# Attention and two dense layers on one core: another way to turn the first two score blocks of the last six jobs

## The chip, the cores and the metric

One core of one Trainium2 chip runs the kernel. The metric is the device time of one execution in microseconds (us), lower being better; the kernel before has a median of 1113.16 us.

## What is computed

```python
def _attn_ref(q, k, v, tau):                  # q, k, v: 4 x 8 x 576 x 64, fp32
    scores = (1.0 / np.sqrt(64)) * np.matmul(q, k.transpose(0, 1, 3, 2))
    thresh = np.max(scores, axis=-1, keepdims=True) - tau
    scores = np.where(scores >= thresh, scores, -1000000000.0)
    scores = scores - np.max(scores, axis=-1, keepdims=True)
    attn = np.exp(scores)
    attn = attn / (np.sum(attn, axis=-1, keepdims=True) + 1e-09)
    return np.matmul(attn, v)
# x = heads joined, 2304 x 512;  then twice  x = g(x @ w_in) @ w_out,  d_ff = 2048
# first g: 0 below -1, (h+1)^2/4 between, h above 1;  second g: h * clip(h + 3, 0, 6) / 6
```

## The kernel before

**Jobs and blocks.** Attention runs in 16 jobs, each a pair of heads of one batch row. The code counts them from 0, so jobs eleven to sixteen are `j` = 10 to 15; this text uses the code's numbers. A job has five blocks of queries: four of 128 per head, and a last one with the 64 remaining queries of both heads. From the moment the first batch row is ready, the matmuls of the first dense layer (`em_h`, line 742, and `em_part`, line 804) are interleaved with the attention steps, so TensorE has two kinds of work in its queue.

**One step of a block.** `em_scores` (line 352) makes the scores on TensorE in two pairs of PSUM banks. VectorE takes them out (line 391): it multiplies by a negative scalar, clips, and gives the row minimum `nm` of the negated scores. `em_exp` (line 398) makes `e = exp(nm - p)` on ScalarE for each head, and then the threshold `th = nm + tau` (line 407) on VectorE. `em_mask` (line 409) compares `p` with `th`, multiplies by `e` and sums, on VectorE (line 413). The masked block must then be turned, keys onto partitions, before the product with v (`pv_chunk`, lines 483 to 502).

**From job 10 on** (`JR = JD = 10`) two things differ. First, the queries and keys come in by strips, are transposed by VectorE in 32 x 32 pieces into a tile `raw` (line 300), split by ScalarE into a rounded part (`qt`, `kt`, line 301) and by GpSimd into the rest (`ql`, `kl`, line 302); scores are the sum of three products. The scale 1/8 is put on with the scalar `taus[:, 3:4]` at line 392. Second, blocks 0 and 1 of a job are turned by `place` (line 426): VectorE transposes 32 x 32 pieces of the block into `pb`, with a strided order of input and output (line 433), and four DMAs per head move the pieces to the tile `Gf` (line 438), 16 DMAs per job. Blocks 2 to 4 are turned by TensorE and copied by ScalarE. `chunk` (line 440) picks the 128 keys of one chunk out of `Gf`; the matmul at line 496 multiplies them with the matching rows of `vn`.

**Buffers.** The tag `w_raw` has three buffers (`RAW = 3`). They hold raw weights, the tiles `raw` and the tiles `kl`. The tag `w_more` has two, for `ql`. `pb` takes the tag `w_c`, two buffers, which the weight preparation also uses. `kt` and `qt` have two buffers each.

**Order.** All DMAs but a few at the start are sent by the queue of SyncE (SP), in order. The plan in `attention` (lines 575 to 690) asks for the queries of job j+1 at block 3 of job j (`unit_q`), for its keys at block 4 (`unit_k`), and for the loads of the next ones behind them. The order within an engine's queue is then fixed by the framework's scheduler when the program is built, from priorities and a timeline that it estimates; in the trace work often runs earlier than the plan names it.

Of the kernel before, what the change touches and what calls it, by code (L numbers as in the profile page):

```python
# [8 lines left out]
F32 = mybir.dt.float32  # L9
# [9 lines left out]
def kernel(  # L19
# [234 lines left out]
    def load_k(j):  # L254
        if j >= NJ:
            return
        b, hp = jobs[j]
        for h in HEADS:
            src = k[b, 2 * hp + h]
            if j >= JT:  # L260
                strips(kn, 2, src, h)
                strips(kn, 0, src[MAIN:SEQ, :], h)
                continue
            nc.sync.dma_start(out=kn[:, 0:4, h * D:(h + 1) * D], in_=rows(src, b))
        if j < JT:
            for r in range(2):
                nc.sync.dma_start(out=kn[r * TAIL:(r + 1) * TAIL, 4, :].rearrange("p (h d) -> p h d", h=2),
                                  in_=both(k, j))
# [24 lines left out]

    def spare(name, tag):
        pool, n = (ap, MORE) if tag == "w_more" else (stage, RAW)
        return pool.tile([128, 1024], F32 if name == "raw" else F32R, tag=tag, name=name, bufs=n)[:, 0:SEQ + TAIL]

    def split_t(nat, hi, name, raw):
        lo = spare(name, "w_more" if name == "ql" else "w_raw")
        V.transpose(out=raw, in_=nat.rearrange("p c n -> p (c n)"))  # L300
        S.activation(out=hi, in_=raw, func=ACTF.Copy)
        G.tensor_tensor(out=lo, in0=raw, in1=f32(hi), op=ALU.subtract)
        return lo
# [3 lines left out]
    def unit_q(j):  # L307
        if j >= NJ or j in qt:
            return
        qt[j] = ap.tile([128, SEQ + TAIL], F32R if j >= JR else F32, tag="qt", name="qt", bufs=2)  # L310
        if j >= JR:
            raws[j] = spare("raw", "w_raw")
            ql[j] = split_t(qn, qt[j], "ql", raws[j])
            load_q(j + 1)
            return
        if j >= JT:
            V.transpose(out=qt[j][:, 0:SEQ], in_=qn.rearrange("p c n -> p (c n)")[:, 0:SEQ])
            if j == JR - 1:
                G.memset(qn[0:64, 4, 64:128], 0.0)
                G.memset(qn[64:128, 4, 0:64], 0.0)  # L320
            load_q(j + 1)
            G.tensor_scalar(out=qt[j][:, 0:SEQ], in0=qt[j][:, 0:SEQ], scalar1=taus[:, 1:2], scalar2=None, op0=ALU.mult)
            return
        tm = unit_bank().rearrange("p e n -> p (e n)")
        for c in range(5):
            turn(tm[:, c * 128:(c + 1) * 128], qn[:, c, :], c == 0)
        load_q(j + 1)
        reads(S.activation(out=qt[j][:, 0:SEQ], in_=tm[:, 0:SEQ], func=ACTF.Copy, scale=taus[:, 1:2]))

    def unit_k(j):  # L330

        if j >= NJ or j in kt:
            return
        kt[j] = ap.tile([128, SEQ + TAIL], F32R if j >= JR else F32, tag="kt", name="kt", bufs=2)
        if j >= JR:
            kl[j] = split_t(kn, kt[j], "kl", raws.pop(j))
            load_k(j + 1)
            return
        if j >= JT:
            V.transpose(out=kt[j], in_=kn.rearrange("p c n -> p (c n)"))  # L340
            load_k(j + 1)
            return
        tm = unit_bank().rearrange("p e n -> p (e n)")
        for i, c in enumerate((4, 0, 1, 2, 3, 4)):
            turn(tm[:, i * 128:(i + 1) * 128], kn[:, c, :], i == 0)
        load_k(j + 1)
        reads(S.activation(out=kt[j], in_=tm[:, 128 - TAIL:128 + MAIN + TAIL], func=ACTF.Copy))
# [4 lines left out]
    def em_scores(j, i):  # L352
# [36 lines left out]
            zt[j] = ap.tile([128, 9], F32, tag="z", name="z", bufs=2)  # L389
        for x, s in enumerate(ss):  # L390
            reads(V.tensor_scalar(out=p[:, x], in0=s[:, :, 0:HS],  # L391
                                           scalar1=taus[:, 3:4] if j >= JR else -1.0, scalar2=3e38,
                                           op0=ALU.mult, op1=ALU.min, accum_out=nm[:, x:x + 1]), len(ss) - 1 - x)
        blk[j, i] = (p, nm, th, [])

# [2 lines left out]
    def em_exp(j, i, x):  # L398
        p, nm, th, es = blk[j, i]
        n = 1 if i == NBLK - 1 else 2  # L400
        if x >= n:
            return
        e = ap.tile([128, 2, HS], F32, tag="e", name="e", bufs=3)
        pins["S"] = S.activation(out=e, in_=p[:, x], func=ACTF.Exp, bias=nm[:, x:x + 1], scale=-1.0)  # L404
        es.append(e)
        if x == n - 1:
            V.tensor_scalar(out=th[:, 0:n], in0=nm[:, 0:n], scalar1=taus[:, 0:1], scalar2=None, op0=ALU.add)

    def em_mask(j, i):
# [16 lines left out]
    def place(j, i):  # L426

        p = p_t[j, i]
        f = turned(j, "a")[0].rearrange("p h c n -> p h (c n)")
        for h in HEADS:  # L430
            p0 = h * (SEQ + TAIL)
            y = stage.tile([128, MAIN], F32, tag="w_c", name="pb", bufs=2)
            V.transpose(out=y.rearrange("p (g c k) -> p g c k", g=4, c=4),  # L433
                        in_=p[:, p0:p0 + MAIN].rearrange("p (c k g) -> p g c k", c=4, g=4))
            for a in range(4):
                c = (4 * i + a) * 128
                E = nc.sync
                E.dma_start(out=f[:, h, c:c + 128], in_=y[32 * a:32 * a + 32, :].rearrange("k (g x) -> k g x", g=4))  # L438

    def chunk(f, j, g, h, c):  # L440
        if j >= JD and g == "a":
            return f[:, h].rearrange("p c n -> p (c n)").rearrange("p (s c n) -> p c s n", c=4, n=32)[:, c]
        return f[:, h, c]

    def rotate():
        mode["r"] = 1 - mode.get("r", 0)
# [36 lines left out]
    def pv_chunk():  # L483

        j, g, c = pvq.pop(0)
        n, d0 = GROUPS[g]
        f, t = gt[g, j]
        if c == 0:
            if j not in xu:
                here.pop(j - XLIVE, None)  # L490
                xu[j] = here[j] = mt.tile([128, SEQ], F32, tag="xu", name="xu", bufs=XLIVE)
            o_t[j, g] = rotate() if mode["mlp"] else bank("Q1")
        o = o_t[j, g][:, 0:n]
        for h in (1, 0):
            with tc.high_priority(offset=0 if h else 900):
                mm = T.matmul(o[h * D:(h + 1) * D], vn[j % 2][:, c, h, :], chunk(f, j, g, h, c) if c < 4 else t,  # L496
                              start=(c == 0), stop=(c == 4), skip_group_check=True)
            after(mm, pe_pins[-1] if h else prev)
            prev = mm
        if c == 4:  # L500
            del gt[g, j], o_t[j, g]
            S.activation(out=xu[j][:, d0:d0 + n], in_=o, func=ACTF.Copy)
# [459 lines left out]
    V.tensor_scalar(out=taus[:, 3:4], in0=taus[:, 2:3], scalar1=0.0, scalar2=3e38, op0=ALU.is_lt, op1=ALU.mult)  # L962
    V.tensor_scalar(out=taus[:, 1:2], in0=taus[:, 2:3], scalar1=0.0, scalar2=0.125, op0=ALU.is_ge, op1=ALU.mult)
    V.tensor_tensor(out=taus[:, 0:1], in0=taus[:, 2:3], in1=taus[:, 3:4], op=ALU.max)
    V.tensor_scalar(out=taus[:, 3:4], in0=taus[:, 1:2], scalar1=-1.0, scalar2=None, op0=ALU.mult)
    warm = [None]

    def warm_up(n):
# [150 lines left out]
```

## Time and profile before

| | us |
|---|---|
| median of three runs | 1113.16 (1112.78 to 1113.59) |
| profiled execution, whole time | 1114.19 |
| its span, first to last instruction | 1112.4 |
| TensorE busy | 1072.6 (96%) |
| VectorE busy | 613.9 (55%) |
| ScalarE busy | 608.4 (55%) |
| GpSimd busy | 453.1 (41%) |

PE is TensorE's matmuls and PEld its weight loads, DVE is VectorE, ACT ScalarE, POOL GpSimd, SPq the queue from which SyncE sends DMAs. The shares are averages over unlike stages: attention with the first dense layer runs to about 445 us, and what comes after it is dense layers alone. The stage of the change is that of jobs 10 to 15, from about 270 to 445 us. An idle time of an engine is put down to the instruction that released it last.

### The profile page before, as it was taken

What the parts mean: (1) busy time and instruction counts of PE and PEld (TensorE: products, weight loads), DVE (VectorE), ACT (ScalarE), POOL (GpSimd) and SP (SyncE); (2) the same over time, 40 slices, a digit from 0 to 9 for tenths busy, and PEclk for the clock granted to TensorE, in tenths of its full rate; (3) what the DMA queues carried; (4) which work ended last, traced back from release to release, by engine and by line L of the source; (5) the groups of instructions that cost most, each with busy time, mean ns of one, the idle gap of its engine ahead of it and who ended that gap; (6) DMA issues with size and microseconds to landing.
All of it is one profiled execution on the core that took longest, in us unless ns stands there. A gap on an engine that the chain in (4) does not pass through costs nothing.

```text
span 1112.4 us, 17797 instructions
## 1 busy us (share of the span) xinstructions
PE 1072.6 (96%) x6466; PEld 880.1 (79%) x6466; DVE 613.9 (55%) x1229; ACT 608.4 (55%) x1203; POOL 453.1 (41%) x390
## 2 busy tenths in 40 slices
PE   7988889999999999999999999999999999999998
PEld 5555567778877788988899888888888888898886
DVE  5889988975889986454437765557411111211111
ACT  5777886876655666565557766645422232333222
POOL 0233767732332312374627566667522222222221
PEclk9999899999999999999999999999999999999999
DMA  6445545332444343143223445533010110010001
GB/s 170 119 96 108 126 115 138 69 86 72 101 98 101 85 106 83 39 121 116 78 76 95 150 147 155 150 120 96 24 38 1 34 39 1 10 39 10 10 1 38
DMA packets 154440, 90.57 MB, mean 81 GB/s; under 512 B 101360, under 2 KB 137456, under 8 KB 154352
## 3 DMA queue, kind: packets, MB, share of 16 engines
q1 hardware_dynamic: 153008, 89.14, 29.8%
q8 instruction: 51, 0.84, 0.3%
q10 hardware_dynamic: 1344, 0.30, 0.1%
q14 instruction: 37, 0.30, 0.1%
HBM read 65.73 MB, written 17.37 MB: 75 GB/s over the span
## 4 chain that ended last, share of the span: by engine, by line
PE 80%; DVE 10%; ACT 3%; issue 2%; SPq 2%; DMA 2%; POOL 1%; DVEq 0%; POOLq 0%; ACTq 0%
PE Q L742 33%; PE P L784 28%; PE Q L804 6%; PE Q L496 5%; PE P L376 4%; DVE p L391 3%; PE Q L290 3%; DVE p L413 3%; DMA Gf<-pb 1%; SPq L438 1%; DVE pb L433 1%; ACT e L404 1%; DVE xl L723 1%; SPq L229 1%; DVE w_c L137 0%
## 5 line engine op out<-in xcount | busy, mean ns | idle before, releaser
L760 POOL TENSOR_TENSOR gl<-r,gh 128x512 fp32r<-128x512 f32 (+1 forms) x190 | 206.6, 1087 | 461.1 <-ACT gh L759 446.4
L742 PE MATMUL Q<-xh,wih 128*128 128x512 f32 (+1 forms) x760 | 260.1, 343 | 1.2 <-DVE r L753 1.1
L742 PE MATMUL Q<-xl,wih 128*128 128x512 f32 (+1 forms) x760 | 256.9, 338 | 0.0
L742 PE MATMUL Q<-xh,wil 128*128 128x512 f32 (+1 forms) x760 | 256.6, 338 | 0.0
L756 DVE SCALAR_TENSOR_TENSOR r<-r,Q 128x512 f32<-128x512 f32 (+1 forms) x80 | 50.7, 633 | 249.4 <-ACT r L755 249.3
L759 ACT ACTIVATE gh<-r 128x512 fp32r<-128x512 f32 (+1 forms) x190 | 99.9, 526 | 138.5 <-PE P L784 53.2
L742 PEld LDWEIGHTS Q<-xh,wih 128*128 128x128 f32 x760 | 144.2, 190 | 22.9 <-issue 2.8
L742 PEld LDWEIGHTS Q<-xl,wih 128*128 128x128 f32 x760 | 144.2, 190 | 15.7
L742 PEld LDWEIGHTS Q<-xh,wil 128*128 128x128 f32 x760 | 144.0, 189 | 15.4
L404 ACT ACTIVATE e<-p,nm 128x576 f32<-128x576 f32 x144 | 109.6, 775 | 49.8 <-DVE p L391 49.3
L413 DVE SCALAR_TENSOR_TENSOR p<-p,th,e 128x576 f32<-128x576 f32 x144 | 125.9, 895 | 14.3 <-ACT e L404 8.3
L755 ACT ACTIVATE r<-Q,three 128x512 f32<-128x512 f32 (+1 forms) x80 | 51.4, 643 | 143.8 <-PE Q L742 140.7
L753 DVE SCALAR_TENSOR_TENSOR r<-r,Q 128x256 f32<-128x256 f32 (+1 forms) x110 | 54.7, 497 | 114.0 <-ACT r L752 112.7
L784 PE MATMUL P<-woh,gh 128*128 128x512 f32 x288 | 111.9, 390 | 0.6 <-DVE ob L842 0.6
L784 PE MATMUL P<-wol,gh 128*128 128x512 f32 x288 | 112.3, 390 | 0.0
L784 PE MATMUL P<-woh,gl 128*128 128x512 f32 x288 | 111.0, 390 | 0.0
L139 POOL TENSOR_TENSOR w_c<-w_c,w_raw 128x512 int32<-128x512 int32 x64 | 89.2, 1394 | 38.1 <-DVE w_c L137 21.7
L290 PE MATMUL Q<-ident,p 128*128 128x128 f32 x560 | 91.8, 282 | 11.6 <-ACT Gf L460 7.0
L376 PE MATMUL P<-kt,qt 64*128 64x288 f32 (+2 forms) x508 | 84.7, 420 | 16.5 <-DVE p L391 14.5
L290 PEld LDWEIGHTS Q<-ident,p 128*128 128x128 f32 x560 | 63.2, 141 | 40.6 <-ACT Gf L460 13.1
L751 ACT ACTIVATE r<-Q,half 128x256 f32<-128x256 f32 (+1 forms) x110 | 58.7, 535 | 41.5 <-PE Q L742 32.7
L804 PE MATMUL Q<-gh,woh 128*128 128x256 f32 x240 | 75.1, 313 | 1.4 <-DVE ob L817 1.4
(107 smaller groups left out, 1978.5 us busy)
## 6 DMA issues: line engine op xcount, KB each, us to landing
w_raw<-in_moe_w_in_dram SPq DMA_DIRECT2D x32, 512.0 KB
w_raw<-in_moe_w_out_dram SPq DMA_DIRECT2D x32, 512.0 KB
Gf<-pb SPq DMA_DIRECT2D x96, 64.0 KB
vn<-in_v_dram SPq DMA_DIRECT2D x32, 128.0 KB
x2p<-ob SPq DMA_DIRECT2D x16, 256.0 KB
x2d<-ob SPq DMA_DIRECT2D x16, 256.0 KB
xst<-x2d SPq DMA_DIRECT2D x16, 256.0 KB
out_dram<-ob SPq DMA_DIRECT2D x16, 256.0 KB
```

Source lines behind the costliest of these rows:

```text
L139: x = G.tensor_tensor(out=c.bitcast(I32), in0=c.bitcast(I32), in1=r, op=ALU.add)
L290: x = T.transpose(out, in_, ident)
L376: mm = T.matmul(o, a[j][r, cs], w[j][r, k0:k0 + HS], start=(n == 0), stop=(n == len(terms) - 1), skip_group_check=True)
L404: pins["S"] = S.activation(out=e, in_=p[:, x], func=ACTF.Exp, bias=nm[:, x:x + 1], scale=-1.0)
L413: pins["M"] = V.scalar_tensor_tensor(out=p[:, x], in0=p[:, x], scalar=th[:, x:x + 1], in1=e, op0=ALU.is_le, op1=ALU.mult, accum_out=zt[j][ ...
L496: mm = T.matmul(o[h * D:(h + 1) * D], vn[j % 2][:, c, h, :], chunk(f, j, g, h, c) if c < 4 else t, start=(c == 0), stop=(c == 4), skip_gro ...
L742: mm = T.matmul(h, l[:, kk * 128:(kk + 1) * 128], r, start=(x == 0), stop=(x == 3 * KD - 1))
L751: S.activation(out=r, in_=h, func=ACTF.Relu, scale=0.5, bias=half)
L759: x = S.activation(out=gh, in_=r, func=ACTF.Copy)
L760: y = G.tensor_tensor(out=gl, in0=r, in1=f32(gh), op=ALU.subtract)
L784: T.matmul(a, l, r, start=(first and x == 0), stop=(last and x == 2))
L804: mm = T.matmul(o, l, r, start=(f == fs[0] and x == 0 and i == 0), stop=(f == fs[-1] and x == 2 and i == 1), skip_group_check=True)
```

## The change

It has four parts, all for jobs 10 to 15.

1. `place` transposes the block without strides. The pieces therefore hold other keys: chunk c of the first group (blocks 0 and 1) now has the keys in another order, and needs rows of v in that order. A second copy of v, `vps`, is loaded for it, by two DMAs per job, into the upper half (columns 512 to 1023) of the job's `raw` tile; the load stands in `unit_k`, behind the load of the next keys.
2. The first of the four `pb` tiles of a job lies in the lower half of the same `raw` tile, and no longer in a `w_c` buffer. The `raw` tile is thereby held until the product with v has read `vps`, where it was free before once `kl` was made.
3. ScalarE multiplies the raw queries by 1/8 in place, before the split; line 391 multiplies by the constant -1.0 in place of the per-partition scalar, and the instruction that made that scalar goes.
4. The threshold `th` is made by ScalarE (`Identity` with a bias), behind the two exponentials, in place of VectorE.

```diff
-        return pool.tile([128, 1024], F32 if name == "raw" else F32R, ...)[:, 0:SEQ + TAIL]
+        return pool.tile([128, 1024], F32, tag=tag, name=name, bufs=n)
-    def split_t(nat, hi, name, raw):
-        lo = spare(name, "w_more" if name == "ql" else "w_raw")
+    vps = {}
+    def split_t(j, nat, hi, name, whole):
+        t = spare(name, "w_more" if name == "ql" else "w_raw")
+        lo = t[:, 0:SEQ + TAIL].bitcast(F32R)
+        raw = whole[:, 0:SEQ + TAIL]
         V.transpose(out=raw, in_=nat.rearrange("p c n -> p (c n)"))
+        if name == "ql":
+            S.activation(out=raw, in_=raw, func=ACTF.Copy, scale=taus[:, 1:2])
         S.activation(out=hi, in_=raw, func=ACTF.Copy)
         G.tensor_tensor(out=lo, in0=raw, in1=f32(hi), op=ALU.subtract)
...
-            kl[j] = split_t(kn, kt[j], "kl", raws.pop(j))
+            kl[j] = split_t(j, kn, kt[j], "kl", raws[j])
             load_k(j + 1)
+            b, hp = jobs[j]
+            vps[j] = raws[j][:, MAIN:2 * MAIN].rearrange("p (h c d) -> p h c d", h=2, c=4)
+            for h in HEADS:
+                nc.sync.dma_start(out=vps[j][:, h], in_=v[b, 2 * hp + h][0:MAIN, :].rearrange("(a c k) d -> k a c d", a=4, c=4))
...
-                                           scalar1=taus[:, 3:4] if j >= JR else -1.0, scalar2=3e38,
+                                           scalar1=-1.0, scalar2=3e38,
...
-        if x == n - 1:
+        if x == n - 1 and j >= JD:
+            S.activation(out=th[:, 0:n], in_=nm[:, 0:n], func=ACTF.Identity, bias=taus[:, 0:1])
+        elif x == n - 1:
             V.tensor_scalar(out=th[:, 0:n], in0=nm[:, 0:n], scalar1=taus[:, 0:1], scalar2=None, op0=ALU.add)
...
-            y = stage.tile([128, MAIN], F32, tag="w_c", name="pb", bufs=2)
-            V.transpose(out=y.rearrange("p (g c k) -> p g c k", g=4, c=4),
-                        in_=p[:, p0:p0 + MAIN].rearrange("p (c k g) -> p g c k", c=4, g=4))
+            if i or h:
+                y = stage.tile([128, MAIN], F32, tag="w_c", name="pb", bufs=2)
+            else:
+                y = raws[j][:, 0:MAIN]
+            V.transpose(out=y, in_=p[:, p0:p0 + MAIN])
...
+    def chunk(j, g, h, c):
+        f, t = gt[g, j]
+        if c == 4:
+            return vn[j % 2][:, c, h, :], t
         if j >= JD and g == "a":
-            return f[:, h].rearrange(...)[:, c]
-        return f[:, h, c]
+            return (vps[j][:, h, c, :],
+                    f[:, h].rearrange("p c n -> p (c n)").rearrange("p (s c n) -> p c s n", c=4, n=32)[:, c])
+        return vn[j % 2][:, c, h, :], f[:, h, c]
...
-    V.tensor_scalar(out=taus[:, 3:4], in0=taus[:, 1:2], scalar1=-1.0, scalar2=None, op0=ALU.mult)
```

## Rows read from the trace of the kernel before

**Rows 1.** Busy time by stretch: length; PE, PEld, DVE, ACT, POOL; clock; DMA share, GB/s.

```profile
303.00:330.00 27.00, 24.66 (x201) 20.80 (x201) 23.42 (x56) 15.87 (x36) 7.17 (x6) 0.94 0.43 98
275.00:411.00 136.00, 126.92 (x1062) 106.97 (x1060) 120.72 (x278) 86.24 (x192) 38.60 (x33) 0.99 0.43 97
411.00:445.00 34.00, 32.62 (x274) 28.22 (x272) 23.40 (x56) 23.15 (x54) 6.22 (x8) 1.00 0.33 88
445.00:1000.00 555.00, 555.00 (x2829) 474.14 (x2826) 229.60 (x316) 266.98 (x477) 254.76 (x205) 1.00 0.24 77
```

**Rows 2.** Waits of TensorE and VectorE, 270 to 445 us: total, times, longest.

```profile
PE P L376 <- DVE p L391: 5.0, 4, 2.3
PE Q L496 <- DMA Gf<-pb: 2.4, 3, 1.0
PE Q L290 <- DVE p L413: 1.0, 2, 0.8
DVE pb L433 <- DMA Gf<-pb: 6.7, 4, 2.1
DVE p L413 <- ACT e L404: 3.9, 7, 1.0
```

**Rows 3.** Timeline of job 11, VectorE and TensorE: start, length, what, idle before.

```profile
317.10 1.08 DVE L433 STREAM_TRANSPOSE pb<-p 128x512 f32<-128x512 f32 x1 [2.15 <-DMA Gf<-pb]
318.93 0.40 PE L376 MATMUL P<-kt,qt 64*128 64x288 f32 x2 [2.34 <-DVE p L391]
```

**Rows 4.** VectorE's groups by shape: busy, mean ns, idle before; 270 to 445 us.

```profile
L391 DVE TENSOR_SCALAR_CACHE_REDUCE p<-P,taus 128x576 f32<-128x576 f32 x54 | 42.1, 808 | 6.0 <-PE Q L290 3.5 <-PE P L376 2.4
L433 DVE STREAM_TRANSPOSE pb<-p 128x512 f32<-128x512 f32 x24 | 26.2, 1111 | 6.7 <-DMA Gf<-pb 6.7
L407 DVE TENSOR_SCALAR th<-nm,taus 128x2 f32<-128x2 f32 x24 | 6.2, 259 | 0.5
L300 DVE STREAM_TRANSPOSE raw<-kn 128x640 f32<-128x640 f32 x5 | 4.2, 839 | 0.9 <-DMA kn<-in_k_dram 0.7 <-issue 0.2
L407 DVE TENSOR_SCALAR th<-nm,taus 128x1 f32<-128x1 f32 x6 | 1.3, 209 | 0.0
```

**Rows 5.** The same groups over the whole run, jobs 0 to 9 among them.

```profile
L391 DVE TENSOR_SCALAR_CACHE_REDUCE p<-P 128x576 f32<-128x576 f32 x90 | 65.2, 751 | 18.9 <-PE Q L290 11.2 <-PE P L376 6.7
L317 DVE STREAM_TRANSPOSE qt<-qn 128x576 f32<-128x576 f32 x6 | 4.6, 772 | 1.1 <-DMA qn<-in_q_dram 1.1
```

**Rows 6.** ScalarE's groups, 270 to 445 us, and its one table load.

```profile
L404 ACT ACTIVATE e<-p,nm 128x576 f32<-128x576 f32 x54 | 41.3, 774 | 22.2 <-DVE p L391 22.1
L474 ACT ACTIVATE Gt<-Q 128x128 f32<-128x128 f32 x26 | 6.9, 267 | 0.9 <-PE Q L290 0.9
L301 ACT ACTIVATE qt<-raw 128x640 fp32r<-128x640 f32 x4 | 2.9, 725 | 0.0
L961 ACT ACT_TABLE_LOAD x1 | 1.3, 1283 | 3.4 <-issue 3.4
```

**Rows 7.** SP's queue: one line's loads, two stretches of job 11, its waits there.

```profile
L277 SPq DMA_DIRECT2D vn<-in_v_dram x14: 372/537/583, 226.6 to 407.2; - x14
...
312.81 5.12 SPq L438 DMA_DIRECT2D Gf<-pb  x8
...
318.67 5.11 SPq L438 DMA_DIRECT2D Gf<-pb  x8
...
SPq L438 <- DVE p L413: 0.6, 1, 0.6
...
SPq L818 <- DVE pb L433: 0.2, 1, 0.2
```

**Rows 8.** Timeline at the change from job 10 to job 11: GpSimd, then TensorE.

```profile
271.46 1.55 POOL L302 TENSOR_TENSOR kl<-raw,kt 128x640 fp32r<-128x640 f32 x1 [1.53 <-ACT kt L301]
295.00 0.30 PE L376 MATMUL P<-kt,ql 128*128 128x288 f32 x1
299.27 0.40 PE L376 MATMUL P<-kt,qt 64*128 64x288 f32 x2
```

More of the change, by code (lines that the diff above doesn't have):

```diff
@@ L295, in spare @@
         pool, n = (ap, MORE) if tag == "w_more" else (stage, RAW)
-        return pool.tile([128, 1024], F32 if name == "raw" else F32R, tag=tag, name=name, bufs=n)[:, 0:SEQ + TAIL]
-    def split_t(nat, hi, name, raw):
-        lo = spare(name, "w_more" if name == "ql" else "w_raw")
+        return pool.tile([128, 1024], F32, tag=tag, name=name, bufs=n)
[4 more added lines that the diff above has]
+        raw = whole[:, 0:SEQ + TAIL]
         V.transpose(out=raw, in_=nat.rearrange("p c n -> p (c n)"))
+        if name == "ql":
+            S.activation(out=raw, in_=raw, func=ACTF.Copy, scale=taus[:, 1:2])
         S.activation(out=hi, in_=raw, func=ACTF.Copy)
@@ L312, in unit_q @@
             raws[j] = spare("raw", "w_raw")
-            ql[j] = split_t(qn, qt[j], "ql", raws[j])
+            ql[j] = split_t(j, qn, qt[j], "ql", raws[j])
             load_q(j + 1)
@@ L431, in place @@
             p0 = h * (SEQ + TAIL)
-            y = stage.tile([128, MAIN], F32, tag="w_c", name="pb", bufs=2)
-            V.transpose(out=y.rearrange("p (g c k) -> p g c k", g=4, c=4),
-                        in_=p[:, p0:p0 + MAIN].rearrange("p (c k g) -> p g c k", c=4, g=4))
+            if i or h:
[3 more added lines that the diff above has]
+            V.transpose(out=y, in_=p[:, p0:p0 + MAIN])
             for a in range(4):
                 c = (4 * i + a) * 128
-                E = nc.sync
-                E.dma_start(out=f[:, h, c:c + 128], in_=y[32 * a:32 * a + 32, :].rearrange("k (g x) -> k g x", g=4))
-    def chunk(f, j, g, h, c):
+                nc.sync.dma_start(out=f[:, h, c:c + 128], in_=y[32 * a:32 * a + 32, :].rearrange("k (g x) -> k g x", g=4))
+    def chunk(j, g, h, c):
+        f, t = gt[g, j]
+        if c == 4:
+            return vn[j % 2][:, c, h, :], t
         if j >= JD and g == "a":
-            return f[:, h].rearrange("p c n -> p (c n)").rearrange("p (s c n) -> p c s n", c=4, n=32)[:, c]
-        return f[:, h, c]
+            return (vps[j][:, h, c, :],
+                    f[:, h].rearrange("p c n -> p (c n)").rearrange("p (s c n) -> p c s n", c=4, n=32)[:, c])
+        return vn[j % 2][:, c, h, :], f[:, h, c]
     def rotate():
@@ L495, in pv_chunk @@
             with tc.high_priority(offset=0 if h else 900):
-                mm = T.matmul(o[h * D:(h + 1) * D], vn[j % 2][:, c, h, :], chunk(f, j, g, h, c) if c < 4 else t,
+                mm = T.matmul(o[h * D:(h + 1) * D], *chunk(j, g, h, c),
                               start=(c == 0), stop=(c == 4), skip_group_check=True)
```

## The prediction

> **What bounds the kernel now.** I read the busy times by stretch first [rows 1]. From 445 to 1000 us TensorE is busy for the whole 555.00 us: nothing that the change does to other engines can show there. In the stretch of the change it isn't: 126.92 of 136.00 us (275 to 411) and 32.62 of 34.00 (411 to 445), so 9.1 + 1.4 = 10.5 us are idle. That is the most that better feeding can give back, and it is small. One thing comes on top: from 303 to 330 the mean granted clock is 0.94 of the upper level (2.4 GHz), against 1.00 in the last two stretches; 6% of 27 us is 1.6 us, which lie in the busy time.
>
> Next the waits [rows 2]: who caused those 10.5 us. 5.0 us are scores that wait for VectorE to empty their PSUM banks (line 391), 1.0 us turns that wait for masks (line 413), and 2.4 us products with v that wait for the last DMA of `place`. The rest (2.1 us) is not touched here. VectorE in its turn stands still for 6.7 us, four times, before the transpose of line 433, because a `pb` buffer is not free until its DMAs have landed. Job 11 shows the chain [rows 3]: the third transpose waits 2.15 us for the first one's buffer, and the scores behind it wait 2.34 us.
>
> So in this stage three queues run close to each other: TensorE busy 93%, VectorE 120.72 of 136 us (89%), and SP, which sends eight DMAs of `place` in 5.12 us (0.64 each) without a gap [rows 7] and whose five waits in job 11's 24.6 us (312.8 to 337.4) add up to 1.7 us only; the first and the last of them are shown. None has much slack.
>
> **The change part by part.** *Transposes without strides.* 24 of them take 1.111 us [rows 4]. Contiguous ones are there in other sizes: 128x640 in 0.839 [rows 4], 128x576 in 0.772 [rows 5]. That is about 1.05 ns a column, so 512 columns would take 0.70; at the worst they take as long as 640, 0.839. I take 0.70: 24 x 0.41 = 9.9 us less on VectorE (6.5 at the least).
>
> *A constant in place of a scalar operand.* Line 391 takes 0.808 with the operand [rows 4] and 0.751 with the constant [rows 5], same shape: 54 x 0.057 = 3.1 us less.
>
> *Thresholds off VectorE.* 24 x 0.259 + 6 x 0.209 = 7.5 us less [rows 4]. The instruction taken away at the start is a single small one off the path of the first job: nothing.
>
> VectorE's sum: 20.5 us less over six jobs, 3.4 us a job of some 27. It would be busy about 76% of the stage.
>
> *ScalarE* gets six scalings of 128x640, near 0.725 each [rows 6], 4.4 us, and 30 thresholds. Their nearest row is a copy of 128x128, 0.267 [rows 6], an upper bound for 128x2; with a bias read for each partition I take no less, 8 us (below it by half at the most). It is busy for 86.24 of 136 us [rows 1], so 12 us over six jobs fit. The place of the thresholds matters more. Both masks of a block need `th`; now `th` is queued behind both exponentials. Until now a first mask could start when `th` was made on VectorE, about 0.26 after the second emptying; now it waits one more exponential (0.774 [rows 6]) and the threshold (0.27): about 0.8 to 0.95 us later, with VectorE's later masks and `place` queued behind it. At five blocks a job that is up to 4.7 us, more than the 3.4 saved, if nothing else stands in between in VectorE's queue. In the trace something often does: masks waited for exponentials in only 7 of 54 cases, 3.9 us [rows 2]. I charge TensorE 1.0 us for all jobs (0 to 5).
>
> *Buffers of `pb`.* With the first tile in `raw`, the third transpose needs the buffer of no DMA in flight; the fourth needs that of the second, whose DMAs are the fifth to eighth in SP's queue. So the stall of 6.7 us goes for the third and a part of it comes back before the fourth. Together with VectorE's relief I let TensorE win 4.5 of the 6.0 us that it waits for lines 391 and 413 (2 to 6), and 1.2 of the 1.6 us of the clock, because that dip is in the stretch with the 2.34 us wait (0 to 1.6).
>
> *The second copy of v.* Two more DMAs a job through SP, shaped like those of `vn`: 0.537 median [rows 7], with the gap between entries some 0.6, 1.2 us a job, 7 us in all. They stand before the `place` DMAs of the same job and wait for GpSimd's `kl`; behind them wait the loads of the next queries, the norm's small DMAs and then `place`. What they cover: SP's idle 1.7 us a job. If that cover holds they cost nothing, if not 1.2 us x 6. I charge 1.0 us (0 to 7). For the last DMA of `place`, which TensorE waits 2.4 us for, the shorter transposes (0.41 each, twice in front of it) work against this; I credit 0.5 (0 to 2.4).
>
> The Trainium skill says (DMA: Bandwidth & Descriptors, section Issuing engines are not separate DMA queues) that the time a sequencer needs to start a DMA is usually small beside the DMA itself. Here the row disagrees: 0.64 us each, and the queue nearly full. By the page the copies of v would be free and the sum below 1.0 us better.
>
> *The `raw` tile is held longer.* Before, `kl` of job 11 was made at 271.46, when job 10 had just begun, and job 11's scores first read it at 299.27 [rows 8]. It needs one of three `w_raw` buffers. With `raw` and `kl` of job 10 and `raw` of job 11 alive there is none until job 10's last scores have been read (end 295.3) or its product with v is done. So `kl` is made at the last moment: 1.55 us of GpSimd plus two hand-overs, some 1.9 us, in the gap between the jobs' scores, which was 4.0 us here (and 2.7, 4.7, 1.2 and 3.3 us at the other four changes of job, by the same lines of the timeline). On these numbers one gap is too short by 0.7 us. I charge 0.5 (0 to 7). The queries' `raw` of job j+2 moves by some 25 us too, with a job left until they are needed. Raw weights of the second phase get their buffers later, but they are used after 445 us, under a TensorE that has no idle time; without that cover some 6 us once.
>
> TensorE's own work doesn't change: the same matmuls, another tile of v.
>
> **Sum** against the profiled execution: -4.5 - 0.5 - 1.2 + 1.0 + 1.0 + 0.5 = -3.7 us. 1114.19 becomes 1110.5. The median of the runs lies 1.03 below that execution, so I predict 1109.5 us, 0.33% less. The whole gain, with no cost, would be 8.4 + 1.6 = 10 us: 1103. All costs at their upper ends without a gain would be 19 us.
>
> **The rivals.** *Exchanged waits.* VectorE's 20.5 us are saved, but it stands as long for thresholds, and SP sets when `place` lands. For it: VectorE's queue is in order, and the delay per block (up to 0.95) times five is more than the saving per job. Against it: masks rarely waited for ScalarE. It decides if VectorE's wait for ScalarE's thresholds comes to more than some 15 us. TensorE's waits stay at about 10 us: 1113.
>
> *The third buffer* (slower). If in front of the late `kl` GpSimd has another split in its queue (the `ql` of the next job, also 1.55), the way from the last scores to the next is 1.9 + 1.55, plus a hand-over, about 3.7 us. Over the five gaps this is 0, 1.0, 0, 2.5, 0.4 us, and once more when GpSimd waits there for ScalarE's double pass of 0.73: some 2 us more at each. 4 to 12 us, less 2 us of gain: 1115 to 1123, middle 1118. It decides from the point at which the way exceeds the gaps' 3.2 us mean. Against it: GpSimd is busy for 38.60 of 136 us only.
>
> *SP becomes the bound* (slower). 1.2 us a job with no slack left makes 7 us, less 3 of gain: 1117. For it: 1.7 us idle a job, waits in order. Against it: some loads can move into other gaps of the queue.
>
> *The change doesn't do what it says:* if a transpose of 128x512 out of this tile costs 1.1 us with or without strides, VectorE saves 10.6 us only and the result is within 0.2% of before; I count it with the first rival.
>
> *Table loads.* The whole run has one load of ScalarE's tables, 1.283 us, for Copy, Exp, Relu, Square and Abs [rows 6]. If `Identity` needed another set than `Exp`, each of 30 blocks would bring two: 77 us on ScalarE, and about 60 us on the path, 1170. The Trainium skill (ScalarE: Activation LUTs, section Table sets: the hidden batching unit) says that identity and the like are filler in every set; by it this doesn't occur. No row here shows `Identity`, and I leave it 1 in 100.
>
> **How the numbers follow.** Forecast (faster) 0.48, exchanged waits 0.27, third buffer 0.13, SP 0.11, tables 0.01. About 0.2%, 2.2 us, is what a measurement can tell from no change. So: faster 0.48, same 0.27, slower 0.25. The range runs from the whole gain, 1103, to the middle of the third buffer's case, 1118; beyond lie the worst part of that case, tables, and a scheduler that orders the stage quite differently. The forecast's own range is 1103 to 1111.
>
> **What would show it.** Line 433 near 0.70 and line 391 near 0.75 on VectorE; no line 407 after 275 us; its busy time from 275 to 411 near 104 us. The wait of line 433 for DMAs below 3 us, TensorE's for line 391 below 2. Masks' wait for thresholds up to 10 us in all is in the sum, beyond 15 it is the first rival. `kl` of job 11 right behind the last scores of job 10; a wait of TensorE's scores for it longer than 1 us at more than one change of job is the third buffer. The prediction is wrong if TensorE's idle time between 275 and 445 us stays above 9 us, or if TensorE is idle after 445 us.

## The result and the profile after

The changed kernel takes 1121.16 us (1119.21 to 1121.71) against 1113.22 us for the kernel before on the same chip: a ratio of 1.0067, 95% interval [1.0054, 1.008]. By the ratio it is slower by 7.5 us, where 3.7 less were forecast. The profiled execution takes 1121.20 us with a span of 1119.2 us, 6.8 more than before.

Seen from TensorE, those 6.8 us are of two kinds. Its matmuls are busy for 1075.0 us in place of 1072.6, and it is idle for 1119.2 - 1075.0 = 44.2 us in place of 39.8. So 4.4 us are new waits, and 2.4 are matmuls that ran longer. The busy times of the same stretches as in [rows 1] (length; PE, PEld, DVE, ACT, POOL; clock; DMA share, GB/s):

```profile
275.00:411.00 136.00, 126.23 (x1046) 104.91 (x1046) 104.35 (x249) 91.61 (x218) 38.74 (x33) 0.99 0.44 100
411.00:445.00 34.00, 30.64 (x246) 24.89 (x242) 18.35 (x48) 19.95 (x48) 4.65 (x5) 0.95 0.41 109
445.00:1000.00 555.00, 555.00 (x2840) 474.42 (x2839) 232.31 (x323) 270.21 (x489) 255.60 (x207) 1.00 0.24 77
```

VectorE was relieved as planned: 104.35 us busy in the first stretch, 16.4 less. TensorE got nothing of it: 9.77 + 3.36 = 13.1 us idle, where it was 10.5 and where the prediction named 9 as the mark above which it would be wrong. From 411 to 445 us the granted clock is now 0.95 of the upper level (2.4 GHz), where it was 1.00; 5% of 34 us is 1.7 of the 2.4 us. From 445 to 1000 us TensorE is without idle time as before. Of the 4.4 us of new waits 2.6 lie in the stage of the change, 0.8 ahead of 270 us and 0.9 behind 1000 us. The engines' groups by shape (busy, mean ns, idle before) show each planned saving:

```profile
L401 DVE TENSOR_SCALAR_CACHE_REDUCE p<-P 128x576 f32<-128x576 f32 x54 | 38.8, 748 | 11.6 <-PE Q L290 6.6 <-PE P L386 4.9
L448 DVE STREAM_TRANSPOSE pb<-p 128x512 f32<-128x512 f32 x18 | 12.5, 696 | 6.5 <-DMA Gf<-pb 6.5
L448 DVE STREAM_TRANSPOSE raw<-p 128x512 f32<-128x512 f32 x6 | 4.2, 705 | 0.0
...
L417 ACT ACTIVATE th<-nm,taus 128x2 f32<-128x2 f32 x24 | 6.9, 286 | 0.0
L306 ACT ACTIVATE raw<-raw,taus 128x640 f32<-128x640 f32 x4 | 3.3, 829 | 0.5 <-DVE raw L304 0.4
```

The lines are those of the changed kernel: 401 is the old 391, 448 the old 433, 417 makes the thresholds, 425 is the mask. The waits from 270 to 445 us (total, times, longest) show where the engines stand now. The last line is of the kernel before, for the fifth:

```profile
DVE p L425 <- ACT th L417: 19.4, 18, 2.0
DVE pb L448 <- DMA Gf<-pb: 6.5, 4, 3.3
PE Q L290 <- DVE p L425: 4.0, 3, 1.6
DVE raw L304 <- DMA rd<-rq: 3.6, 1, 3.6
PE Q L759 <- DVE r L770: 3.2, 2, 1.9
PE Q L290 <- ACT Gf L477: 2.3, 2, 1.9
PE P L386 <- DVE p L401: 1.9, 3, 1.4
PE Q L513 <- DMA Gf<-pb: 1.6, 1, 1.6
...
PE Q L742 <- DVE r L753: 0.3, 1, 0.3
```

In [rows 2] the masks waited for ScalarE's exponentials for 3.9 us; now they wait 19.4 us for its thresholds. TensorE's wait for line 401 did shrink (5.0 to 1.9), but turns wait for masks 4.0 us (1.0 before), and the first dense layer (line 759, the old 742) waits 3.2 us for its input from VectorE (0.3 before). The next timeline, of job 15 (start, length, what, idle before), is one such case: first VectorE, then ScalarE.

```profile
428.86 0.71 DVE L448 STREAM_TRANSPOSE pb<-p 128x512 f32<-128x512 f32 x1 [3.27 <-DMA Gf<-pb]
429.50 0.72 DVE L401 TENSOR_SCALAR_CACHE_REDUCE p<-P 128x576 f32<-128x576 f32 x1
430.15 0.75 DVE L401 TENSOR_SCALAR_CACHE_REDUCE p<-P 128x576 f32<-128x576 f32 x1
432.48 0.82 DVE L425 SCALAR_TENSOR_TENSOR p<-p,th,e 128x576 f32<-128x576 f32 x1 [1.57 <-ACT th L417]
...
430.26 0.77 ACT L414 ACTIVATE e<-p,nm 128x576 f32<-128x576 f32 x1 [2.89 <-DVE p L401]
430.95 0.65 ACT L127 ACTIVATE w_c<-w_raw 128x512 f32<-128x512 f32 x1
431.50 0.76 ACT L414 ACTIVATE e<-p,nm 128x576 f32<-128x576 f32 x1
432.16 0.28 ACT L417 ACTIVATE th<-nm,taus 128x2 f32<-128x2 f32 x1
```

`nm` is complete when the second emptying ends, near 430.9. The threshold comes at 432.4, behind an exponential, a piece of weight preparation and another exponential, and VectorE stands still for 1.57 us. Just before, it had stood for 3.27 us in front of the fourth transpose of `place`.

The longest of VectorE's waits stands in front of a transpose of keys. SP first, then VectorE, and last the same transpose in v_act, a run below in which SP sends no copies of v:

```profile
354.58 4.06 SPq L229 DMA_DIRECT2D kn<-in_k_dram  x8
358.74 2.27 SPq L347 DMA_DIRECT2D raw<-in_v_dram  x2
361.11 1.55 SPq L539 DMA_DIRECT2D rd<-rq  x4
...
361.89 0.84 DVE L304 STREAM_TRANSPOSE raw<-kn 128x640 f32<-128x640 f32 x1 [3.58 <-DMA rd<-rq]
...
363.00 0.85 DVE L304 STREAM_TRANSPOSE raw<-kn 128x640 f32<-128x640 f32 x1 [3.09 <-DMA rd<-rq]
```

The two copies of v (line 347) follow the keys' loads in SP's order, and without them VectorE waits there for 3.09 us all the same. So this wait is not theirs.

The start of each job's first transpose of `place`, and the end of the last product with v, place the loss (us, read from the two timelines):

| | job 10 | 11 | 12 | 13 | 14 | 15 | end |
|---|---|---|---|---|---|---|---|
| before | 281.3 | 309.1 | 336.0 | 362.7 | 390.7 | 415.4 | 447.2 |
| after | 282.2 | 308.3 | 335.6 | 364.1 | 395.1 | 418.2 | 453.1 |

Until job 12 next to nothing is lost. From 13 to 15 it is, and the rest of the run is carried along (+5.9 at the end of attention, +6.8 at the end).

### The profile page after: what moved, and what is told of

It is laid out like the page before. It is cut to its first block, busy times and chain, and to the rows that moved or that the text cites. A ratio compares the mean times of both kernels' runs of the same rounds, so it can differ in the third digit from the quotient of the medians.

```text
span 1119.2 us, 17823 instructions
## 1 busy us (share of the span) xinstructions
PE 1075.0 (96%) x6466; PEld 879.3 (79%) x6466; DVE 594.5 (53%) x1198; ACT 617.0 (55%) x1239; POOL 450.7 (40%) x390
## 4 chain that ended last, share of the span: by engine, by line
PE 76%; DVE 9%; ACT 4%; DMA 3%; SPq 3%; issue 3%; POOL 1%; DVEq 0%; ACTq 0%; POOLq 0%
PE Q L759 32%; PE P L801 28%; PE Q L821 5%; PE Q L513 4%; PE P L386 4%; DVE p L401 3%; DVE p L425 3%; PE Q L290 3%; SPq L451 1%; ACT e L414 1%; DMA Gf<-pb 1%; SPq L229 1%; DMA qn<-in_q_dram 1%; DMA w_raw<-in_moe_w_out_dram 1%; DVE xl L740 1%
## 5 line engine op out<-in xcount | busy, mean ns | idle before, releaser
L425 DVE SCALAR_TENSOR_TENSOR p<-p,th,e 128x576 f32<-128x576 f32 x144 | 129.9, 927 | 28.3 <-ACT th L417 20.2
L401 DVE TENSOR_SCALAR_CACHE_REDUCE p<-P 128x576 f32<-128x576 f32 x144 | 104.0, 750 | 31.3 <-PE Q L290 18.8
L768 ACT ACTIVATE r<-Q,half 128x256 f32<-128x256 f32 (+1 forms) x110 | 58.6, 534 | 39.8 <-PE Q L759 30.9
```

Source lines behind the costliest of these rows:

```text
L401: reads(V.tensor_scalar(out=p[:, x], in0=s[:, :, 0:HS], scalar1=-1.0, scalar2=3e38, op0=ALU.mult, op1=ALU.min, accum_out=nm[:, x:x + 1]), ...
L425: pins["M"] = V.scalar_tensor_tensor(out=p[:, x], in0=p[:, x], scalar=th[:, x:x + 1], in1=e, op0=ALU.is_le, op1=ALU.mult, accum_out=zt[j][ ...
L768: S.activation(out=r, in_=h, func=ACTF.Relu, scale=0.5, bias=half)
```

## The experiments

The expectations of the first runs weigh two explanations, **T** (the thresholds) and **H** (the held `raw` tile). Later ones split them into four. **E**: any hand-over of the thresholds from ScalarE to the masks costs. **P**: only their place behind both exponentials costs. **R**: the `raw` tile held until the product with v makes the keys late. **S**: two more loads a job through SP's queue delay what stands behind them. Ratios are to the kernel before on the same chip, with 95% intervals; kernels built on "before" have its other parts unchanged.

One thing limits the comparisons. Each kernel is built anew, and the build may put the same work in another order. In the built programs TensorE's queue has the same 5946 instructions, but another one stands at 28 places between copy_act and turns_act, at 70 between copy_act and copy_only, at 527 between v_act_th_vector and th_vector, and at 905 between th_vector and the change. A small count makes a comparison nearly one of the named part alone; with a large one the price holds the other order too.

**th_vector**: the change, with the thresholds made by VectorE again.

```diff
-        if x == n - 1 and j >= JD:
-            S.activation(out=th[:, 0:n], in_=nm[:, 0:n], func=ACTF.Identity, bias=taus[:, 0:1])
-        elif x == n - 1:
+        if x == n - 1:
             V.tensor_scalar(out=th[:, 0:n], in0=nm[:, 0:n], scalar1=taus[:, 0:1], ...)
```

> The changed kernel with the thresholds back on VectorE, nothing else. Theory T (the 20.2 us that VectorE's masks wait for ScalarE's thresholds are the loss): 1112 to 1115 us, VectorE's wait of masks back below 6 us. Theory H (the raw tile that is held, and what comes late through it: kl, raw weights, loads): stays at 1119 to 1122 us.

Measured 1.0038 [1.0023, 1.0053]: taking the thresholds back takes away 0.29% (3.2 us) of the change's loss, and 0.38% stays.

**th_only**: before, with part 4 alone (the reverse of that diff).

> The kernel before with the thresholds of jobs 10 to 15 on ScalarE, nothing else. Theory T: 1118 to 1122 us. Theory H: 1112 to 1115 us, since VectorE's waits are covered by what TensorE has queued.

Measured 1.0113 [1.0096, 1.013], 12.6 us: slower than the whole change. VectorE's largest wait, 270 to 445 us:

```profile
DVE p L415 <- ACT th L407: 16.1, 18, 1.5
```

**th_mid**: the change, with the threshold asked for between the two exponentials.

```diff
+        if x == n - 1 and j >= JD:
+            S.activation(out=th[:, 0:n], in_=nm[:, 0:n], func=ACTF.Identity, bias=taus[:, 0:1])
         pins["S"] = S.activation(out=e, in_=p[:, x], func=ACTF.Exp, ...)
```

> The changed kernel with the threshold on ScalarE still, but asked for between the two exponentials and no longer behind both. Theory P (it is the place in ScalarE's queue that costs): as good as with the thresholds on VectorE, 1114 to 1118 us, masks' wait for thresholds below 8 us. Theory E (any hand-over of thresholds from ScalarE costs as much): 1119 to 1122 us.

Measured 1.0073 [1.0052, 1.0095]. The masks' wait for thresholds halves, with 3.8 us for exponentials beside it, and no time comes of it. P fails its own forecast; but TensorE's order differs from the change's at 1186 places, so what the place alone is worth isn't shown.

```profile
DVE p L425 <- ACT th L414: 8.9, 14, 1.8
DVE p L425 <- ACT e L416: 3.8, 4, 1.4
```

**copy_only**: before, with a second copy of v (keys in the old order) loaded through SP into the held `raw` tile and read by the products; transposes strided as before, all `pb` tiles as before.

```diff
+            vps[j] = raws[j][:, MAIN:2 * MAIN].rearrange("p (h c d) -> p h c d", h=2, c=4)
+            for h in HEADS:
+                nc.sync.dma_start(out=vps[j][:, h], in_=v[b, 2 * hp + h][0:MAIN, :].rearrange("(c p) d -> p c d", c=4))
```

> The kernel before with a second copy of v (in the old order of keys) loaded into the upper half of the raw tile and read from there by the products of the first group, so that raw is held as in the change and SP sends two more loads a job; strided turns, thresholds and scaling as before, all four pb tiles in w_c. Theory H: 1118 to 1123 us, with kl made only behind the last scores of the job before. Theory T: 1112 to 1115 us.

Measured 1.0047 [1.0032, 1.0062], 5.2 us.

**copy_act**: the same with `nc.scalar.dma_start`, so that ScalarE's queue sends these two loads.

> The kernel copy_only (the kernel before with a second copy of v in raw), its two extra loads a job sent by ScalarE's queue in place of SP's. Theory R (raw is held too long, kl and raw weights come late): 1116 to 1120 us like copy_only. Theory S (SP's full queue is the cost): 1112 to 1115 us.

Measured 1.0001 [0.999, 1.0012]. The `raw` tile is held as long and the keys' rest is made as late as in the changed kernel (job 11, GpSimd; the first fence is copy_act, the second the change; [rows 8] has 271.46), yet nothing is lost. R falls, S stands.

```profile
296.27 1.55 POOL L306 TENSOR_TENSOR kl<-raw,kt 128x640 fp32r<-128x640 f32 x1 [2.36 <-PE P L384]
```

```profile
295.61 1.83 POOL L308 TENSOR_TENSOR kl<-raw,kt 128x640 fp32r<-128x640 f32 x1 [2.25 <-PE P L386]
```

**loads_only**: before, plus two SP loads a job (the second of half the size) into columns of `raw` that nothing reads; `raw` is not held.

```diff
+            for h in HEADS:
+                nc.sync.dma_start(out=spots[h], in_=v[b, 2 * hp + h][0:MAIN // (1 + h), :].rearrange("(c p) d -> p c d", p=128))
```

> The kernel before with two more loads a job through SP, at the place where the change has them, into columns of raw that nobody reads, so that raw is free soon again; the second load is half as large. Theory S: 1116 to 1120 us. Theory R: 1112 to 1115 us, kl made as early as before.

Measured 1.0015 [1.0004, 1.0026]. So two more loads in SP's queue do not cost copy_only's 5.2 us by their number alone: here they follow an early `kl`, and one is half as large. That copy_only's cost comes from loads that wait for a late `kl`, with other DMAs behind them in SP's order, fits but isn't shown: SP stands in front of them for 2.0 us only, and the profiled executions of copy_only and copy_act are equally long (1116.68 and 1116.64), so their traces don't show where the 5 us arise.

```profile
SPq L345 <- POOL gl L771: 2.0, 2, 1.7
```

**scale_only**: before, with part 3 alone (scaling on ScalarE, the constant in line 391).

```diff
+        if name == "ql":
+            S.activation(out=raw, in_=raw, func=ACTF.Copy, scale=taus[:, 1:2])
-                                           scalar1=taus[:, 3:4] if j >= JR else -1.0, ...
+                                           scalar1=-1.0, ...
```

> The kernel before with the raw queries scaled by ScalarE and the constant at the emptying of the scores, nothing else. Both theories: 1111 to 1114 us; VectorE's emptying at 0.75 us each, 3.1 us less in all, little of it on TensorE's path.

Measured 1.0016 [1.0007, 1.0026]: no gain from 3.1 us less on VectorE. TensorE's order differs from that of before at 836 places, so a small gain could be hidden in it.

**abs_pinned_th_vector**: th_vector, with the instruction of line 127 (weight preparation) held behind the one before it in its group, which itself stands behind an exponential.

```diff
-            S.activation(out=f32(c), in_=f32(t[:, :, 1]), func=ACTF.Abs)
+            after(S.activation(out=f32(c), in_=f32(t[:, :, 1]), func=ACTF.Abs), x)
```

> The changed kernel with thresholds on VectorE, and the raw weights' absolute value on ScalarE (line 127) tied behind the operation ahead of it, so that it can't stand in ScalarE's queue at the end of attention and wait there for a buffer or for weights. If that wait (4.6 us of ScalarE at 430 and 438 us in the kernel with thresholds on VectorE) is a part of what the held raw tile costs: 1113 to 1116 us. If it is covered: 1116 to 1118 us as without.

Measured 1.0053 [1.0032, 1.0073], not better than th_vector: ScalarE's waits for raw weights don't show in the time.

**turns_act**: copy_act with unstrided transposes (part 1 of the change, the loads through ScalarE's queue).

```diff
-            V.transpose(out=y.rearrange("p (g c k) -> p g c k", g=4, c=4),
-                        in_=p[:, p0:p0 + MAIN].rearrange("p (c k g) -> p g c k", c=4, g=4))
+            V.transpose(out=y, in_=p[:, p0:p0 + MAIN])
```

> Before plus the second copy of v (loads sent by ScalarE's queue, copy in the held raw tile) plus transposes without strides; the queries are scaled as before, thresholds are on VectorE, all pb tiles in the two buffers of before. It differs from copy_act (1.0001 [0.999, 1.0012]) in the strides alone. Transposes should take 0.70 us, 24 x 0.41 = 9.9 us less on VectorE. Theory 'VectorE's relief reaches TensorE' (the prediction's first term): 2 to 5 us faster than before, 0.995 to 0.998. Theory 'the relief is exchanged for the wait on pb's buffers and DMAs, whatever is done with the thresholds': the wait of the transposes for the DMAs of Gf rises by 4 us or more from some 7 us, and the time is within 0.2% of before.

Measured 0.9991 [0.9982, 1.0001], against copy_act's 1.0001. The transposes fall from 1111 to 701 ns, 24 x 0.41 = 9.8 us of VectorE's time; 1.1 us of the total may come of it, which these intervals don't separate from nothing. The groups of copy_act and of turns_act, 270 to 445 us:

```profile
L441 DVE STREAM_TRANSPOSE pb<-p 128x512 f32<-128x512 f32 x24 | 26.3, 1111 | 2.4 <-DMA Gf<-pb 2.4
...
L399 DVE TENSOR_SCALAR_CACHE_REDUCE p<-P,taus 128x576 f32<-128x576 f32 x54 | 42.3, 812 | 14.9 <-PE Q L290 9.7 <-PE P L384 5.1
```

```profile
L441 DVE STREAM_TRANSPOSE pb<-p 128x512 f32<-128x512 f32 x24 | 16.6, 701 | 4.8 <-DMA Gf<-pb 4.4 <-DVE r L763 0.2
...
L399 DVE TENSOR_SCALAR_CACHE_REDUCE p<-P,taus 128x576 f32<-128x576 f32 x54 | 42.1, 811 | 12.2 <-PE Q L290 8.1 <-PE P L384 4.0
```

In copy_act VectorE waits 14.9 us for TensorE before its emptyings, where it waited 6.0 in [rows 4]: it had time to spare, so the 1.1 us hold for this base, and the kernel before may have had more to gain. (The profiled execution of copy_act, 1116.64, is also the slowest of its ten; their median is 1113.29.) Where most of the freed time goes is one more line of each, copy_act first: VectorE waits longer for ScalarE in the first dense layer.

```profile
DVE r L764 <- ACT r L763: 3.4, 6, 1.1
...
DVE r L763 <- ACT r L762: 9.4, 8, 2.9
```

**v_act_th_vector** and **v_act**: th_vector, and the change itself, with the copies of v sent by ScalarE's queue.

```diff
-                nc.sync.dma_start(out=vps[j][:, h], ...
+                nc.scalar.dma_start(out=vps[j][:, h], ...
```

> The changed kernel with the thresholds back on VectorE and the copies of v sent by ScalarE's queue; scaling on ScalarE and the first pb tile in raw stay. If the two costs found are separate and add (thresholds 4 us in the change, SP's queue 4.9 us between copy_only and copy_act), 1121.2 - 4.0 - 4.9 = 1112.3, 0.999 of before. If the copies' cost through SP was there only because the stage with strided transposes had no slack elsewhere, it stays near th_vector's 1.0038 (1117). If the full relief of VectorE now reaches TensorE, as predicted for the change, 1108 to 1110 (0.995 to 0.997).

> The changed kernel with only the queue of the copies of v changed: ScalarE's in place of SP's. Theory 'two separate costs': 1121.2 - 4.9 = 1116, about 1.003 of before; masks still wait some 15 to 20 us for the thresholds. Theory 'thresholds alone, SP is covered beside them': 1120 to 1122, 1.006 to 1.008. VectorE's wait for the keys' loads (3.6 us at 362) should be gone in either case.

Measured 0.9994 [0.9985, 1.0002] and 1.0069 [1.0056, 1.0082]. With the thresholds on VectorE the other queue is worth 0.44% (4.9 us); with them on ScalarE it is worth nothing. One thing expected of v_act failed: VectorE's wait for the keys did not go (3.1 us after 3.6, shown above). v_act_th_vector is the best form of the change and can't be told from before, although in its profiled execution (1110.29, the fastest of eleven) TensorE is idle for 5.6 + 0.9 = 6.4 us only:

```profile
275.00:411.00 136.00, 130.44 (x1093) 108.53 (x1092) 110.22 (x287) 92.27 (x202) 37.30 (x34) 1.00 0.47 106
411.00:445.00 34.00, 33.12 (x271) 27.40 (x270) 20.31 (x53) 22.68 (x54) 7.13 (x9) 1.00 0.33 88
```

**th_twice**: before, with VectorE's thresholds kept and used, and the 30 instructions on ScalarE besides, for a tile that nothing reads: ScalarE's load without the hand-over. **th_thrice** has them twice. **th_twice_pool** has them once, as additions on GpSimd.

```diff
+        if x == n - 1 and j >= JD:
+            td = ap.tile([128, 2], F32, tag="td", name="td", bufs=2)
+            S.activation(out=td[:, 0:n], in_=nm[:, 0:n], func=ACTF.Identity, bias=taus[:, 0:1])
```

> Before, with VectorE's thresholds kept and used, plus the same 30 instructions on ScalarE that write a tile that nothing reads: ScalarE's load of th_only without the hand-over. Theory 'it is the hand-over from ScalarE to the masks': same as before, within 0.2%. Theory 'it is ScalarE's time and the order of the work that comes of it': 8 to 12 us slower, as th_only was (1.0113). An end near 1.004 would mean both.

> Before, with VectorE's thresholds kept and used, plus 60 instructions on ScalarE that write tiles that nothing reads (th_twice has 30). Theory 'ScalarE's time is on the path': the loss about doubles, 14 to 18 us (1.013 to 1.016). Theory 'the order of the work by chance': no proportion, anywhere between 0 and 12 us.

> Before, with VectorE's thresholds kept and used, plus the 30 additions on GpSimd into a tile that nothing reads. Theory 'ScalarE's time': same as before within 0.2%, since GpSimd is busy 28% of the stage. Theory 'any 30 more instructions make the build order the stage another way, and that costs': 3 to 9 us slower, near th_twice's 1.0081.

Measured 1.0081 [1.0067, 1.0096], 1.0063 [1.0046, 1.008] and 1.0007 [0.9998, 1.0016]. So a loss comes without any hand-over: the program with 0.28 us more on ScalarE for each of 30 blocks is 9 us slower, the one with the same additions on GpSimd is not, and twice the time doesn't cost more. But the order differs with it. In the built programs th_twice has TensorE's 5946 instructions in another order at 721 places and th_thrice at 596; th_twice_pool has them in exactly the order of before. Whether ScalarE's time or the order costs the 9 us, these three can't tell.

**th_pool**: before, with the thresholds really made by GpSimd, without ScalarE's queue in between. **v_act_th_pool**: the change with GpSimd's thresholds and ScalarE's queue for the copies.

```diff
-            S.activation(out=th[:, 0:n], in_=nm[:, 0:n], func=ACTF.Identity, bias=taus[:, 0:1])
+            G.tensor_scalar(out=th[:, 0:n], in0=nm[:, 0:n], scalar1=taus[:, 0:1], scalar2=None, op0=ALU.add)
```

> Before, with the thresholds made by GpSimd in place of VectorE: a hand-over to the masks as in th_only, but through a queue that does not hold the exponentials. Theory 'ScalarE's time': 0 to 4 us slower (the hand-over's own part, 12 less 9). Theory 'any hand-over of the thresholds': 10 to 13 us slower, like th_only (1.0113).

> The changed kernel with the copies of v sent by ScalarE's queue and the thresholds made by GpSimd. v_act_th_vector is 0.9994 [0.9985, 1.0002]. VectorE is relieved of another 7.5 us. Theory 'VectorE's relief reaches TensorE when ScalarE's queue is spared': 1108 to 1110, 0.995 to 0.998. Theory 'it is exchanged for other waits': within 0.2% of before; by the hand-over theory it is 4 us or more slower.

Measured 1.0084 [1.0063, 1.0105] and 1.0046 [1.0034, 1.0059]. A hand-over from an engine with time to spare comes out nearly as slow. Here too the order differs, at 997 places from that of before in th_pool and at 571 from that of v_act_th_vector in v_act_th_pool, so these runs don't show the hand-over's price by itself. The masks' and the scores' waits in th_pool:

```profile
PE P L376 <- DVE p L391: 8.8, 5, 3.9
DVE p L415 <- POOL th L407: 7.6, 13, 1.7
DVE p L415 <- ACT e L404: 4.1, 5, 1.1
```

**th_only_order**: th_only, with the instructions of all five queues held in the order that the build gave them before; only the thresholds change queue, each right behind the second exponential. **after_order**: the whole change, with TensorE's instructions alone held so.

```diff
+        for a, b in zip(full, full[1:]):      # full: one engine's instructions in the order of before
+            tc.add_manual_dep(b, a.name, mybir.DependencyInfo(mybir.DependencyClass.NoSync, ...))
```

> Before with the thresholds on ScalarE (as th_only, 1.0113), but the instructions of all five queues are held to the order that the build gave them before; only the 30 thresholds change queue, each right behind the second exponential. Theory 'the order': within 0.2% of before, up to 3 us for the masks' waits of some 0.5 us each. Theory 'the hand-over and ScalarE's time': 9 to 13 us slower again, masks waiting 15 us or more for thresholds.

> The whole change, with TensorE's instructions alone held to the order that the build gave them before the change; the other queues are ordered by the build as it likes. Theory 'the order': the 8 us of loss go, 1109 to 1114 (0.997 to 1.001). Theory 'the hand-over and the held tile': as slow as the change, 1.005 to 1.009, or slower, since TensorE's order doesn't suit the later thresholds and keys.

Measured 1.0064 [1.0044, 1.0085] and 1.0052 [1.0032, 1.0073]. With the order held the thresholds still cost 7.1 of the 12.6 us; this part is made on the chip, by ScalarE's time and the hand-over together. The intervals of th_only and th_only_order don't meet, so the other order of the work (999 places) costs some 5 us more. In the whole change the middle values leave 1.7 us to the order, and the intervals of 1.0067 and 1.0052 overlap. The masks' and turns' waits in th_only_order:

```profile
DVE p L416 <- ACT th L407: 24.7, 23, 2.3
PE Q L290 <- DVE p L416: 5.5, 5, 2.0
```

## Why the prediction was wrong

Put in a row, the runs lead from the kernel before to the change by one part after the other. Beyond turns_act each step also changes TensorE's order at 500 places or more:

| step | ratio | its price, us |
|---|---|---|
| copy of v through ScalarE's queue, `raw` held (copy_act) | 1.0001 | 0.1 |
| + unstrided turns (turns_act) | 0.9991 | -1.1 |
| + scaling on ScalarE, first `pb` in `raw` (v_act_th_vector) | 0.9994 | 0.3 |
| + the copies through SP (th_vector) | 1.0038 | 4.9 |
| + thresholds on ScalarE (the change) | 1.0067 | 3.2 |
| the last two in the other order: thresholds (v_act), then SP | 1.0069, 1.0067 | 8.3, -0.2 |

Prices are differences of ratios times 1113.2 us; those below 1.5 us are not separate from nothing.

**The savings on the engines: right.** 0.696 and 0.705 us for the transposes (0.70 forecast), 0.748 for line 401 (0.751), 104.35 us of VectorE in the stretch (104), 0.28 to 0.29 for a threshold (0.27). The Trainium skill says that identity is in every set of ScalarE's tables as filler (ScalarE: Activation LUTs, section Table sets: the hidden batching unit). The trace of the changed kernel agrees: thresholds by `Identity` stand between exponentials, with one table load in the whole run.

```profile
L978 ACT ACT_TABLE_LOAD x1 | 1.3, 1283 | 3.4 <-issue 3.4
```

**"I let TensorE win 4.5": wrong; this was nearly the whole gain.** turns_act takes 9.8 us from VectorE and TensorE wins about 1 us of it. Nor does scale_only's 3.1 us bring anything, which come with six scalings on ScalarE (829 ns each, where 725 were taken). The 6.0 us that TensorE waits for VectorE in [rows 2] were thus not a share of its load. The time that a shorter transpose frees goes into other waits of VectorE: in turns_act it waits 6.0 us longer than in copy_act for ScalarE in the first dense layer and 2.0 longer for `pb`. The step that failed is the one from VectorE's busy time to TensorE's waits.

**The stall of `pb`: half right.** The third transpose's wait is gone, and "a part of it" was to come back before the fourth. All of it did: 6.5 us after 6.7, where less than 3 was forecast. Earlier transposes meet the same DMAs: while VectorE stands for 3.27 us in job 15, SP sends this row.

```profile
422.82 9.26 SPq L451 DMA_DIRECT2D Gf<-pb  x12
```

**"I charge TensorE 1.0 us" for the thresholds: the term that decided.** The mechanism was written down (one more exponential and the threshold in front of each first mask, up to 4.7 us a job) and then discounted, because in the trace masks waited for ScalarE in 7 of 54 cases. That count was of the old order, in which the first mask needed the first exponential alone. It told how rarely ScalarE was late for what it had to deliver then, not for what it has to deliver now. The wait came to 19.4 us, 18 times. Its price is 12.6 us alone, 7.1 with the order of the work held, and 8.3 on top of v_act_th_vector, where the order differs at 1218 places.

**"What they cover: SP's idle 1.7 us a job": wrong.** The copies' price was set at 1.0 with 7 as the upper end. It is 4.9 to 5.2 us where nothing else holds the stage up (the 5.2 nearly without another order, 70 places), and nothing beside the thresholds (v_act against the change, 862 places), so the two prices don't add. The rule of the Trainium skill against which this was weighed (DMA: Bandwidth & Descriptors, section Issuing engines are not separate DMA queues), that the time to start a DMA is usually small beside the DMA itself, is no guide here: the copies' sends take 0.648 us at the least, 0.656 in the median, and the same two loads cost 5 us in one queue and none in the other.

```profile
L347 SPq DMA_DIRECT2D raw<-in_v_dram x12: 648/656/1577, 189.8 to 411.2; - x12
```

**The late keys (0.5): right.** copy_act has them as late and loses nothing; the third-buffer rival fell with it.

**The clock (-1.2): wrong in sign.** A second stretch below the upper level came, 411 to 445 us, which costs the 1.7 us of above. TensorE had been idle twice there, for VectorE both times, and then the clock stood at the lower level (1.2 GHz, 0.50) for a while; the last rows are 2 us each, in the columns of [rows 1]:

```profile
430.96 0.40 PE L386 MATMUL P<-kt,qt 64*128 64x288 f32 x2 [1.40 <-DVE p L401]
...
434.19 0.30 PE L290 MATMUL Q<-ident,p 128*128 128x128 f32 x1 [1.61 <-DVE p L425]
...
433.00:435.00 2.00, 0.81 (x4) 0.60 (x6) 2.00 (x8) 0.72 (x3) 0.00 (x0) 0.93 0.17 39
435.00:437.00 2.00, 2.00 (x12) 1.23 (x10) 0.97 (x4) 1.72 (x4) 0.72 (x1) 0.50 0.00 0
437.00:439.00 2.00, 2.00 (x14) 1.08 (x10) 1.32 (x4) 0.25 (x1) 0.00 (x0) 0.72 0.00 0
```

This is so beyond the profiled execution. Over the whole span the mean granted clock of the change's four executions is 0.989, 0.989, 0.986 and 0.989; that of the 83 executions of the kernel before beside the experiments is 0.992 on average. An estimate from these, 0.004 of 1119 us, puts some 4 of the 7.5 us down to the clock. Where falls follow waits, as in these rows, a wait is paid once while TensorE stands and in part again behind it. It is not the cost of every run: th_thrice has 0.9915 on average, the kernel before beside it 0.9919, and it is 7.0 us slower.

**The rivals.** The first, exchanged waits, had the right sign to look for: it was to decide from 15 us of masks' wait, and 19.4 came. Its time, 1113, was wrong, since it let the saved 20.5 us pay for the wait. The saving was worth about 1 us, the wait 3 to 8. SP as the bound has its price confirmed (5 us of the 7 named) but not as the only cause. The range ended at 1118 because two costs that each lay inside their bounds were never set against a gain of nearly nothing: -1 + 5 + 3 gives 7 us more than before.

**What stays open.** Why 30 idle instructions on ScalarE cost 9 us and 60 no more was not settled: neither th_twice nor th_pool was run with the order held. So the runs don't show how the thresholds' 7.1 us divide between ScalarE's time and the hand-over, nor that either costs by itself. Nor do they show where in the stage the copies of v in SP's queue cost their 5 us.

## What to carry to other kernels

Count an engine's relief only where the trace shows that engine last, and price a moved instruction by the chain that it joins, however short it is and however idle the engine is on average. A wait count of the old order says nothing about a new dependency. Where two costs may share one slack, measure each with and without the other before adding or dismissing one. Where the build may reorder the rest, compare the orders, or hold them, before putting a difference down to the part that was changed.

## What the runs showed of the hardware

A 32 x 32 transpose of 128x512 with strided input and output takes 1.111 us, without strides 0.70. The queue made a difference where the load didn't: two DMAs a job cost 5.2 us from SP and 0.1 from ScalarE (copy_only, copy_act). Thirty thresholds on ScalarE, 0.28 us each on an engine that is busy for 63% of the stage [rows 1], made the whole slower by 7.1 us with every queue's order held (th_only_order). TensorE's clock fell to its lower level behind two waits of 1.40 and 1.61 us, about 1.7 us lost.
